# Sliding-window attention and a squared-ReLU MLP on one core: a sixth up-projection by Strassen's algorithm, softmax division on either of two engines, drawn offsets in the planner's priorities

## The chip, the cores and the metric

The kernel runs on one core of a Trainium2 chip. The metric is device microseconds for one execution. TensorE (PE in the profile) multiplies matrices into PSUM, VectorE (DVE) and ScalarE (ACT) do the elementwise work, GpSimd (POOL) issues the loads of inputs and SyncE (SP) issues transposing DMAs and stores.

## What is computed

For 8 batches, 8 heads, 576 positions and head size 64, causal attention with a window of 128 and a bias that falls off linearly with distance; its output, 4608 tokens of 512 numbers, goes through an MLP:

```python
scores = np.where(mask, scale * q @ k.T + bias, -1e9)
attn = np.exp(scores - scores.max(-1, keepdims=True))
x = (attn / attn.sum(-1, keepdims=True)) @ v       # heads side by side: 4608 x 512
h = x @ w_in                                       # 512 -> 2048
out = np.maximum(h, 0.0) ** 2 @ w_out              # 2048 -> 512
```

## The kernel before, in words

**Attention.** Each batch is cut into 5 blocks of queries (128, 128, 128, 128, 64), 40 blocks in all, numbered m. For a block the keys and queries are loaded and transposed (`prepare`), TensorE makes the scores against this block and the one before it (`scores`, line 529), ScalarE takes the exponential (line 566), VectorE multiplies by a table of masks and biases (lines 575 and 582), and TensorE multiplies by the values (`values`, line 609). The values carry a 65th column of ones, so the sum of each row's exponentials comes out beside the result. A "half" of a block is 4 heads: VectorE takes the reciprocals of the 4 sums (line 632), and `norm` multiplies the 4 x 64 columns by them (line 637), PSUM to the bf16 tile `x`. From block 13 on a DMA on SP's queue transposes `x` into the ring `xT` (line 651), which holds four groups of 512 tokens.

**MLP.** The tokens make 9 groups of 512, numbered g from 0. An up-projection of a group is either plain (`fc_step`, 16 steps of 4 matmuls with 512 columns each, line 710; ScalarE's ReLU, line 723; the square on either engine) or by Strassen's algorithm (`fast_unit`, 4 units of 7 products, each product 4 matmuls with 256 columns, line 784). Strassen's form needs sums of weight blocks (`weight_sums`, line 378, made once), sums of token blocks (`token_sums`, line 753, four subtractions into the one buffer `T`), and more elementwise work on the products: three copies by ScalarE to fp32 (lines 844, 854, 865), three additions by VectorE (lines 850 and 818), two ReLUs from PSUM by ScalarE (line 812) and two from SBUF on either engine (lines 823 and 825). `FAST` names the groups that use it: 4 to 8. The down-projections of groups 1 to 8 all go by Strassen's algorithm (`product`, 7 x 16 = 112 matmuls with 256 columns, line 935), on sums of blocks (`sums`, line 896). Group 0's is plain (line 1014).

**Order.** Nothing is ordered by hand. Each piece of work is a `Task` with a key, the engines that may take it with a cost for each, its dependencies, and the buffers and PSUM banks that it takes and frees. `Plan.order` simulates the engines: the next task is the one that can start first, with the lower priority number in front among those that can start at once (on VectorE and ScalarE, among those that can start within 100 ns of the first). A task that two engines may take goes to the one that reaches it first. The result fixes the order on each engine's queue in the program. The priority is the key plus an optional shift for the task's group (its function's name and its rounded key):

```python
t.prio = t.key + (shift.get(t.group, 0.0) if shift else 0.0)
```

Before the change `order` is called without shifts. One stage, in which the down-projection of group g runs beside the up-projection of group g + 1 and the attention for later groups, is 128 keys long. Loads of the first weights and blocks have keys below -100000; those of the later blocks about -500000.

Of the kernel before, what the change touches and what calls it, by code (L numbers as in the profile page):

```python
# [2 lines left out]

# [7 lines left out]
AF = mybir.ActivationFunctionType  # L11
# [189 lines left out]
def kernel(  # L201
    ctx: ExitStack, tc: tile.TileContext, q, k, v, moe_w_in, moe_w_out, out
):
    nc = tc.nc

    B, H, S, D = q.shape
# [3 lines left out]
    scale = 1.0 / (D ** 0.5)  # L210
# [6 lines left out]
    NG = NT // 512  # L217
# [7 lines left out]
    PLAIN = 1  # L225
    EARLY = 0.92
    WIDE = NKB
    FAST = range(NG - 5, NG)
    RING = 4 * 512

    const = ctx.enter_context(tc.tile_pool(name="const", bufs=1))
# [11 lines left out]
    def ring(name, n, shape):  # L243
        return [const.tile(shape, BF16, name=f"{name}_{i}") for i in range(n)]
# [8 lines left out]
    xt = ring("x", size["x"], [128, d_model])  # L253
    x_sums = ring("T", size["T"], [128, 3, d_model])

    plan = Plan({"rec": 4, "rt": 3, "g": 2, "S": 2, "osb": 4,
                 "s1": 1, "u2": 1, "x1": 1, "fs": 1, "fu": 2, "fx": 1, **size},
                {"h": 3, "o": 3, "a": 4, "f": 5, "t": 3})

    def bank_tile(sl, name, dtype=FP32):  # L260
        return psum.tile([128, 512 if dtype == FP32 else 1024], dtype, tag=f"bank{sl.idx}", bufs=1, name=name)

    def act(n):
        return n * 0.836 + 50.0

    def dve(n, rate=1):
        return n / rate / 0.96 + 68.0

    def mm(n):
        return max(n, 64) / 2.4 + 4.0  # L270
# [45 lines left out]
    def place(h):  # L316
        c, half = divmod(h, 2)
        return 4 * (c // 2) + 2 * half + c % 2
# [50 lines left out]
    def weight_sums(n, key):  # L369
        w = w_in_sb.rearrange("p (c k) (j r f) -> p c r k j f", c=2, r=2, f=128)  # L370
        a11, a12, a21, a22 = (w[:, c, r, :, 2 * n:2 * n + 2] for r in range(2) for c in range(2))
        s1, s2, s3, s4 = (w_sum[:, i, :, 2 * n:2 * n + 2] for i in range(4))
        last = None
        for o, a, b, op in ((s1, a21, a22, ALU.add), (s2, s1, a11, ALU.subtract),
                            (s3, a11, a21, ALU.subtract), (s4, a12, s2, ALU.subtract)):
            def emit(o=o, a=a, b=b, op=op):
                for k in range(2):
                    nc.vector.tensor_tensor(o[:, k], a[:, k], b[:, k], op=op)
            last = plan.add({"DVE": 2 * dve(256, 2)}, key, emit, [t_win[n], last, t_read[2][0]])
        t_wsum[n] = last  # L380
# [46 lines left out]
    def copy(task, o, i):  # L427
        if task.eng == "DVE":
            nc.vector.tensor_copy(o, i)
        else:  # L430
            nc.scalar.activation(o, i, AF.Copy)
# [68 lines left out]
    def bank_of(m, h):  # L500
        c, half = divmod(h, 2)
        return (0 if packed(m) else 2 * (c // 2)) + half
# [83 lines left out]
    def values(m):  # L586
        b, kb = divmod(m, NKB)
        sk, n, kb, due = prep_of[m]
        parts, sP, t_P = score_of[m]
        p0 = parts[0][0]  # L590
        first = b == 0
        x_by_dma = m >= X_DMA
        both = {"ACT": act(C * n), "DVE": dve(C * n, 2)}

        sx = Slot("x")
        t_norm = []
        for hf in range(2):
            slot_v = Slot("t")
            last = None

            def value_bank(slot_v=slot_v):
                slot_v.tile = bank_tile(slot_v, "pv")
            for hi in range(4):
                h = 4 * hf + hi
                for part, mk in parts:
                    def emit(h=h, hi=hi, part=part, mk=mk, slot_v=slot_v):
                        if slot_v.tile is None:
                            value_bank(slot_v)
                        nc.tensor.matmul(  # L609
                            slot_v.tile[:, hi * (D + 1):(hi + 1) * (D + 1)],  # L610
                            Pt[sP.idx][:, place(h), part, :], vt[s_in[mk, "v"].idx][:, h, :],
                            start=part == p0, stop=part == 1)
                    rel = []
                    if hf == 1 and hi == 3:
                        if part == 0 or kb == NKB - 1:
                            rel.append(s_in[mk, "v"])
                        if part == 1:
                            rel.append(sP)
                    new = hi == 0 and part == p0
                    last = plan.add({"PE": mm(D + 1)}, due - 12 + 4 * hf, emit,  # L620
                                    [last, t_P[bank_of(m, h)], t_in[mk, "v"]]
                                    + ([t_P[bank_of(m, 4 * hf + i)] for i in range(4)] + chain["pv"] if new else []),
                                    ([slot_v] + ([sx] if hf == 0 else [])) if new else [], rel)
                    if new:
                        last.pad = functools.partial(value_bank, slot_v), slot_v
            chain["pv"] = [last]
            srec = Slot("rec")

            def rec(slot_v=slot_v, srec=srec):
                srec.tile = work.tile([128, 4], FP32, tag="rec", bufs=4, name="rec")  # L630
                pv = slot_v.tile[:, 0:4 * (D + 1)].rearrange("p (h e) -> p h e", h=4)
                nc.vector.reciprocal(srec.tile[0:n, :], pv[0:n, :, D])
            t1 = plan.add({"DVE": 97.0}, due - 12 + 4 * hf, rec, [last], [srec])

            def norm(slot_v=slot_v, srec=srec, hf=hf):
                pv = slot_v.tile[:, 0:4 * (D + 1)].rearrange("p (h e) -> p h e", h=4)
                nc.vector.tensor_tensor(  # L637
                    xt[sx.idx][0:n, hf * 256:(hf + 1) * 256].rearrange("p (h e) -> p h e", h=4),
                    pv[0:n, :, 0:D],
                    srec.tile[0:n, :].unsqueeze(2).to_broadcast([n, 4, D]),  # L640
                    op=ALU.mult)
            t_norm.append(plan.add({"DVE": dve(256)}, due - 12 + 4 * hf, norm, [t1] + t_norm,
                                   [], [slot_v, srec]))
        t0 = b * S + kb * 128
        if x_by_dma:
            cut = [0, n] if t0 // RING == (t0 + n - 1) // RING else [0, RING - t0 % RING, n]

            def turn_x():
                for lo, hi in zip(cut, cut[1:]):
                    c0 = (t0 + lo) % RING  # L650
                    nc.sync.dma_start_transpose(xT[:, :, c0:c0 + hi - lo], xt[sx.idx][lo:hi, :])
            t_xT[b, kb] = plan.add({"SP": 1280.0 * (len(cut) - 1)}, due, turn_x, t_norm, [], [sx], dma=900.0)
        else:
            slot_x = Slot("t")
            last = None
            for c in range(C):
                def x_bank():
                    slot_x.tile = bank_tile(slot_x, "xp", BF16)

                def emit(c=c):  # L660
                    if slot_x.tile is None:
                        x_bank()
                    nc.tensor.transpose(slot_x.tile[:, c * 128:(c + 1) * 128],  # L663
                                        xt[sx.idx][:, c * 128:(c + 1) * 128], ident)
                last = plan.add({"PE": mm(128)}, due, emit, [last] + t_norm,
                                [slot_x] if c == 0 else [], [sx] if c == C - 1 else [])
                if c == 0:
                    last.pad = x_bank, slot_x

            def evac():  # L670
                copy(t_xT[b, kb], xT[:, :, t0 % RING:t0 % RING + n],
                     slot_x.tile[:, 0:512].rearrange("p (c t) -> p c t", c=C)[:, :, 0:n])
            t_xT[b, kb] = plan.add(both if first else {"DVE": both["DVE"]}, due, evac, [last], [], [slot_x])

    sk_of, t_kq_of, prep_of = {}, {}, {}
    m = 0
    while m < NBLK:
        ms = [m, m + 1] if m % NKB == NKB - 1 and MERGE <= m < NBLK - 1 else [m]
        for m in ms:
            prep_of[m] = prepare(m)  # L680
        scores(ms)
        for m in ms:
            values(m)
        m += 1
# [350 lines left out]
    for g in range(NG):  # L1035
        base = key
        if g == 2:
            for n in range(4):
                weight_sums(n, base + 64 * n)
        if g and g + 1 in FAST:  # L1040
            t_of = token_sums(g + 1, base - 60)
# [14 lines left out]
            if g * 512 < lo + blk[kb] and g * 512 + 512 > lo:  # L1056
                t.deps += t_read[g]

    done = plan.order()
    kernel.plan = done  # L1060
    with tc.manual_schedule():
        clear = 0.0
        for t in done:
            if t.eng == "PE":
                if t.start < plan.FILL and t.pad:
                    bank, slot = t.pad
                    n = round((t.start - clear) / 107.0) if t.start < plan.HOT else int(0.75 * (t.start - clear) / 56.0)
# [39 lines left out]
```

## Time and profile before

| | |
|---|---|
| median of 3 runs | 296.42 us (296.12 to 296.74) |
| the profiled execution's own time | 294.85 us |
| its span, from the first instruction to the last | 293.1 us |
| granted TensorE clock | 1.000 |
| PE, DVE, ACT busy, share of the span | 97%, 85%, 77% |

A row of the windows view gives a stretch of the span, its length, and then for each engine the busy time in it and the number of instructions, the granted clock, and the mean share of the DMA engines and what they moved. A row of a group of instructions gives line, engine, operation, output and inputs, shapes and count, then the busy time of the group and the mean duration of one in ns, then the engine's idle time ahead of them. A row of the chain that ended last gives start, length, and the work with its count. Matmuls overlap: the duration of one is longer than the distance from one to the next.

### The profile page before, as it was taken

To read this page: it belongs to the slowest core of one execution; us is meant where nothing else is said; L and a number is where in the kernel's file an instruction comes from. 1 tells how busy PE (TensorE), PEld (TensorE's weight loads), DVE (VectorE), ACT (ScalarE), POOL (GpSimd) and SP (SyncE) were. 2 spreads that over 40 slices of the span, in tenths; PEclk is the share of its full clock that TensorE was granted. 3 is DMA by queue.
4 is the path that set the end of the run, shared out by engine and by line. 5 is a ranking of instruction groups with operands and counts; after the bars stand their busy time and mean duration, and the time that the engine had idled before them with its cause. 6 is when DMAs were issued, how large, how long until landed. Compare 5 with 4: busy or idle time off the path is not lost.

```text
span 293.1 us, 8500 instructions
## 1 busy us (share of the span) xinstructions
PE 284.0 (97%) x3377; PEld 230.6 (79%) x3393; DVE 248.3 (85%) x663; ACT 227.0 (77%) x430; POOL 105.5 (36%) x131
## 2 busy tenths in 40 slices
PE   7899999999999999999999999999999999999995
PEld 6798977765666675667988888888888888888884
DVE  6967996895998757867999999899999999989923
ACT  6658998976789839878888988998889788589620
POOL 8947758824825635433714273422000000000000
PEclk9999999999999999999999999999999999999999
DMA  9999999999999999999999999999973040301223
GB/s 135 179 189 161 166 185 170 171 124 196 173 141 211 149 147 218 144 174 185 168 155 111 142 203 139 169 138 197 25 110 92 8 68 29 107 2 36 73 74 107
DMA packets 169944, 39.36 MB, mean 134 GB/s; under 512 B 157104, under 2 KB 169392, under 8 KB 169904
## 3 DMA queue, kind: packets, MB, share of 16 engines
q0 software_dynamic: 114656, 18.10, 96.8%
q1 hardware_dynamic: 54192, 20.46, 37.5%
q8 instruction: 26, 0.43, 0.6%
q10 hardware_dynamic: 1056, 0.26, 0.4%
q14 instruction: 14, 0.11, 0.2%
HBM read 36.70 MB, written 9.44 MB: 157 GB/s over the span
## 4 chain that ended last, share of the span: by engine, by line
PE 76%; DMA 12%; DVE 5%; ACT 3%; issue 2%; POOL 1%; SPq 0%; POOLq 0%; ACTq 0%
PE o L935 31%; PE f L784 19%; PE h L710 13%; DMA kq<-in_k_dram 6%; PE pv L609 5%; DMA w_in_sb<-in_moe_w_in_dram 4%; PE ps_s L529 4%; PE o L1014 4%; DMA raw<-in_k_dram 1%; ACT rt L812 1%; POOL vt L415 1%; ACT g L835 1%; DVE rt L818 1%; ACT P L566 1%; PE xp L663 1%
## 5 line engine op out<-in xcount | busy, mean ns | idle before, releaser
L566 ACT ACTIVATE P<-ps_s 128x512 bf16<-128x512 f32 (+1 forms) x130 | 68.8, 600 | 11.8 <-PE ps_s L529 11.8
L710 PE MATMUL h<-xT,w_in_sb 128*128 128x128 bf16 (+2 forms) x501 | 66.3, 270 | 1.3 <-issue 0.5
L415 POOL DMA_DIRECT2D vt<-in_v_dram x40 | 34.0, 853 | 76.6 <-PE pv L609 56.9
L935 PEld LDWEIGHTS <-g 128*128 128x128 bf16 x512 | 49.3, 98 | 8.8
L723 ACT ACTIVATE rt<-h 128x512 bf16<-128x512 f32 x64 | 37.7, 606 | 13.3 <-PE h L710 12.4
L710 PEld LDWEIGHTS <-w_in_sb 128*128 128x128 bf16 x512 | 38.7, 98 | 10.3 <-DMA w_in_sb<-in_moe_w_in_dram 0.6
L582 DVE TENSOR_TENSOR P<-P,masks 128x1024 bf16<-128x1024 bf16 x56 | 38.2, 684 | 4.2 <-ACT P L566 4.0
L935 PEld LDWEIGHTS <-S 128*128 128x128 bf16 x384 | 36.6, 98 | 6.3
L415 POOL DMA_DIRECT2D kq<-in_k_dram x39 | 33.7, 864 | 17.5 <-DMA kqT<-kq 12.1
L935 PE MATMUL o<-w_mix,S 128*128 128x256 bf16 x256 | 37.6, 273 | 0.2 <-issue 0.2
L935 PE MATMUL o<-w_out_sb,g 128*128 128x256 bf16 x256 | 37.1, 273 | 0.0
L935 PE MATMUL o<-w_mix,g 128*128 128x256 bf16 x256 | 36.9, 273 | 0.0
L784 PEld LDWEIGHTS <-w_sum 128*128 128x128 bf16 x320 | 30.9, 98 | 5.2 <-issue 0.9
L415 POOL DMA_DIRECT2D kq<-in_q_dram x39 | 33.7, 865 | 2.4 <-PE pv L609 1.2
L637 DVE TENSOR_TENSOR x<-pv,rec 128x256 bf16<-128x256 f32 (+1 forms) x80 | 33.0, 416 | 0.9
L812 ACT ACTIVATE rt<-f 128x512 bf16<-128x512 f32 x40 | 24.1, 602 | 8.5 <-PE f L784 7.5
L609 PE MATMUL pv<-vt,P 128*128 128x65 bf16 x576 | 29.6, 193 | 0.9 <-DVE P L575 0.7
L609 PEld LDWEIGHTS <-P 128*128 128x128 bf16 x576 | 25.2, 97 | 6.5 <-DVE P L575 1.5
L784 PE MATMUL f<-xT,w_in_sb 128*128 128x256 bf16 x160 | 26.0, 273 | 0.0
L784 PEld LDWEIGHTS <-w_in_sb 128*128 128x128 bf16 x240 | 22.7, 98 | 3.4
L784 PE MATMUL f<-xT,w_sum 128*128 128x256 bf16 x160 | 24.2, 272 | 0.5 <-ACT fu L854 0.5
L784 PE MATMUL f<-T,w_sum 128*128 128x256 bf16 x160 | 24.2, 272 | 0.0
(76 smaller groups left out, 475.0 us busy)
## 6 DMA issues: line engine op xcount, KB each, us to landing
out_dram<-osb SPq DMA_DIRECT2D x35, 256.0 KB, 3.8
vt<-in_v_dram POOLq DMA_DIRECT2D x32, 128.0 KB, 6.0
kq<-in_k_dram POOLq DMA_DIRECT2D x31, 128.0 KB, 6.3
kq<-in_q_dram POOLq DMA_DIRECT2D x31, 128.0 KB, 6.7
w_in_sb<-in_moe_w_in_dram POOLq DMA_DIRECT2D x4, 512.0 KB, 9.3
w_out_sb<-in_moe_w_out_dram POOLq DMA_DIRECT2D x4, 512.0 KB, 9.1
kq<-in_k_dram POOLq DMA_DIRECT2D x8, 64.0 KB, 8.1
kq<-in_q_dram POOLq DMA_DIRECT2D x8, 64.0 KB, 8.0
```

What stands on the lines that cost most here:

```text
L415: nc.gpsimd.dma_start(o, src[b, :, kb * 128:kb * 128 + n, :].rearrange("h s d -> s h d"))
L529: nc.tensor.matmul(slots[bank_of(m, 2 * c + half)].tile[:, 0:cpb * n * len(parts)].rearrange("p (c t q) -> p c t q", c=cpb, t=len(parts))[ ...
L566: nc.scalar.activation(view(Pt[sP.idx]), src, AF.Exp, bias=0.0, scale=scale)
L582: nc.vector.tensor_tensor(pt, pt, mk, op=ALU.mult)
L609: nc.tensor.matmul(slot_v.tile[:, hi * (D + 1):(hi + 1) * (D + 1)], Pt[sP.idx][:, place(h), part, :], vt[s_in[mk, "v"].idx][:, h, :], star ...
L637: nc.vector.tensor_tensor(xt[sx.idx][0:n, hf * 256:(hf + 1) * 256].rearrange("p (h e) -> p h e", h=4), pv[0:n, :, 0:D], srec.tile[0:n, :]. ...
L710: nc.tensor.matmul(slot.tile[:, f * w:(f + 1) * w], w_in_sb[:, cc, (fc + f) * 128:(fc + f + 1) * 128], xT[:, cc, g * 512 % RING + lo:g * 5 ...
L723: nc.scalar.activation(srt.tile, slot.tile, AF.Relu, bias=0.0, scale=1.0)
L784: nc.tensor.matmul(bank[name].tile[:, jj * 256:jj * 256 + 256], w, m, start=opens and jj == 0 and k == 0, stop=k == 1, skip_group_check=True)
L812: nc.scalar.activation(srt.tile, bank[name].tile, AF.Relu, bias=0.0, scale=1.0)
L935: nc.tensor.matmul(bank[t].tile[:, t * 256:(t + 1) * 256], left(g, what, j)[:, t * 128:(t + 1) * 128], right(by, j), start=opens and j == ...
L1014: nc.tensor.matmul(bank.tile, g_slots[g].tile[:, fc, t * 128:(t + 1) * 128], w_out_sb[:, fc], start=fc == 0, stop=fc == FCB - 1)
```

## The change

`FAST` begins at group 3 instead of group 4, so the up-projection of group 3 goes by Strassen's algorithm too. `norm` may be planned on ScalarE for blocks from m = 5 on: there it is four activations of 64 columns, each with a column of reciprocals as its scale, planned at 4 x (64 x 0.836 + 50) = 414 ns against 335 ns on VectorE. And each group of tasks whose rounded key is above -100000 gets a shift, drawn evenly between -8 and 8 keys with a fixed seed.

```diff
-    FAST = range(NG - 5, NG)
+    FAST = range(NG - 6, NG)
...
             def norm(slot_v=slot_v, srec=srec, hf=hf):
                 pv = slot_v.tile[:, 0:4 * (D + 1)].rearrange("p (h e) -> p h e", h=4)
+                if t_norm[hf].eng == "ACT":
+                    for h in range(4):
+                        nc.scalar.activation(xt[sx.idx][0:n, (4 * hf + h) * D:(4 * hf + h + 1) * D], pv[0:n, h, 0:D],
+                                             AF.Copy, scale=srec.tile[0:n, h:h + 1])
+                    return
                 nc.vector.tensor_tensor(
...
-            t_norm.append(plan.add({"DVE": dve(256)}, due - 12 + 4 * hf, norm, [t1] + t_norm,
+            t_norm.append(plan.add({"DVE": dve(256), "ACT": 4 * act(64)} if m >= WIDE else {"DVE": dve(256)}, due - 12 + 4 * hf, norm, [t1] + t_norm,
                                    [], [slot_v, srec]))
...
-    done = plan.order()
+    spread = random.Random(355)
+    done = plan.order({g: spread.uniform(-8.0, 8.0) for g in sorted({t.group for t in plan.tasks if t.group[1] > -100000})})
```

More of the change, by code (lines that the diff above doesn't have):

```diff
@@ L1 @@
 import functools
+import random
 from contextlib import ExitStack
```

## The prediction

> **What bounds the kernel now.** I read the page first: the busy times, then the chain of work that ended last.
>
> ```profile
> span 293.1 us, 8500 instructions
> PE 284.0 (97%) x3377; PEld 230.6 (79%) x3393; DVE 248.3 (85%) x663; ACT 227.0 (77%) x430; POOL 105.5 (36%) x131
> PE 76%; DMA 12%; DVE 5%; ACT 3%; issue 2%; POOL 1%; SPq 0%; POOLq 0%; ACTq 0%
> ```
>
> TensorE is busy for 284.0 of 293.1 us and makes 76% of the chain. The 12% of DMA are the wait for weights and first blocks (rows in the third part). Busy is not the same as full, because a matmul's recorded end lies after the next one's start. So I cut the trace into stages, at every 112th matmul of line 935 (a down-projection is 112 of them): stage g runs from the first product of group g to that of group g + 1. The windows view gives:
>
> ```profile
> core 0: us, PE busy (x) PEld busy (x) DVE busy (x) ACT busy (x) POOL busy (x), PEclk, DMA share, GB/s
> 74.60:106.20 31.60, 30.97 (x336) 21.55 (x341) 27.12 (x89) 25.03 (x47) 17.26 (x21) 1.00 1.81 170
> 106.20:137.90 31.70, 31.33 (x342) 21.05 (x345) 23.77 (x62) 24.25 (x47) 12.57 (x15) 1.00 1.96 173
> 137.90:167.30 29.40, 29.36 (x362) 25.16 (x360) 28.95 (x73) 25.28 (x49) 11.70 (x14) 1.00 1.77 142
> 167.30:197.40 30.10, 29.65 (x363) 25.23 (x361) 28.94 (x76) 26.84 (x53) 12.59 (x15) 1.00 1.67 161
> 197.40:226.70 29.30, 29.25 (x362) 25.06 (x361) 28.79 (x75) 25.95 (x51) 1.57 (x2) 1.00 0.85 108
> ```
>
> Stages 1 and 2 (31.6 and 31.7 us) hold plain up-projections, of groups 2 and 3; stages 3, 4 and 5 (29.4, 30.1, 29.3) hold Strassen's. The clock is 1.00 throughout. VectorE has 7.9 us to spare in stage 2 (31.70 - 23.77) and about 0.5 to 1.2 in stages 3 to 5; ScalarE has 7.4 us to spare in stage 2 and 3.3 to 4.1 in stages 3 to 5. To see how full TensorE is I need the distance between matmuls, which long unbroken pieces of the chain give, and the counts in each stage.
>
> ```profile
> 106.14 3.38 PE o L935 x31
> 112.73 2.16 PE h L710 x10
> 138.27 1.75 PE f L784 x16
> 70.87 0.59 PE pv L609 x16
> 70.32 0.55 PE ps_s L529 x16
> 109.53 0.56 PE ps_s L529 x24
> ```
>
> A matmul with 256 columns takes 0.109 us (3.38 / 31, and 1.75 / 16), one with 512 columns 0.216, one with values 0.037, and a burst of scores 0.55 whether it has 16 records or 24. The counts below are, in order, line 935 and line 710 in stage 2, line 784 in stage 3 (the number after PEld's busy time is complete where PE's lacks some records, and a product or two straddle a boundary), the values of line 609 in stages 2 to 5, and the scores of line 529 in stages 2 to 5.
>
> ```profile
> 106.20:137.90 31.70, 15.05 (x115) 10.52 (x113) 1.00 1.96 173
> 106.20:137.90 31.70, 16.33 (x59) 5.83 (x64) 1.00 1.96 173
> 137.90:167.30 29.40, 16.12 (x112) 10.71 (x112) 1.00 1.77 142
> 106.20:137.90 31.70, 3.52 (x72) 3.03 (x72) 1.00 1.96 173
> 137.90:167.30 29.40, 3.27 (x64) 2.86 (x64) 1.00 1.77 142
> 167.30:197.40 30.10, 3.21 (x64) 2.79 (x64) 1.00 1.67 161
> 197.40:226.70 29.30, 3.86 (x72) 3.16 (x72) 1.00 0.85 108
> 106.20:137.90 31.70, 3.12 (x96) 2.26 (x96) 1.00 1.96 173
> 137.90:167.30 29.40, 2.49 (x72) 1.81 (x72) 1.00 1.77 142
> 167.30:197.40 30.10, 2.49 (x72) 1.80 (x72) 1.00 1.67 161
> 197.40:226.70 29.30, 2.27 (x64) 1.64 (x64) 1.00 0.85 108
> ```
>
> The 96 scores are 3 bursts of 16 and 2 of 24, the 72 are 3 and 1, the 64 are 4 and none. Stage 2 then needs 112 x 0.109 + 64 x 0.216 + 72 x 0.037 + 5 x 0.55 = 12.2 + 13.8 + 2.7 + 2.75 = 31.45 us of its 31.7. Stage 3 needs 12.2 + 12.2 + 2.4 + 2.2 = 29.0 of 29.4, stage 4 the same of 30.1, stage 5 12.2 + 12.2 + 2.7 + 2.2 = 29.3 of 29.3. So TensorE's own work is the bound; unfilled are 0.25, 0.4, 1.1 and 0 us, 1.75 us in these four stages.
>
> **The change, first part: group 3 by Strassen.** Stage 2 loses 64 matmuls of 0.216 (13.8 us) and gets 112 of 0.109 (12.2): -1.6 us of TensorE, needing 29.85. This lies on the path that sets the end. What could take it back is the elementwise work, for VectorE and ScalarE then carry what they carry in stages 3 to 5, where VectorE is all but full. Those stages leave 0.4, 1.1 and 0 us unfilled, 0.5 on average, so I take 30.35 for stage 2, which is **-1.35 us**; with 0 unfilled it is -1.85, with 1.1 -0.75.
>
> Two steps are moved with it. The weight sums are now needed at about 106 us rather than 138. The token sums of group 3 are four more subtractions, which stand between the landing of its last tokens and its first product; those of group 4 can no longer run ahead, because `T` is then held by group 3.
>
> ```profile
> L378 DVE TENSOR_TENSOR w_sum<-w_in_sb,w_sum x8: 276/285/285, 79.8 to 89.5; 128x256 bf16<-128x256 bf16 x8
> L753 DVE TENSOR_TENSOR T<-xT,T x10: 413/417/423, 133.4 to 253.2; 128x512 bf16<-128x512 bf16 x10
> 105.60 3.93 PE o L935 x36
> POOL vt L415 <- PE pv L609: 56.9, 14, 8.4
> ```
>
> The weight sums are done by 90 us: 16 us of cover, no cost. The token sums are not so well covered: from 105.60 on TensorE runs 36 down-projection products in a row, with no up-projection between them, so group 3's tokens come just in time, and 4 x 0.417 = 1.7 us are added behind them. The cover is the 112 products of group 2, of which 76 would still be left; I cost it at nothing, and at +1.7 us if the cover runs out (first part then +0.3). That the loads could not follow speaks little: GpSimd waited 56.9 us for value buffers that TensorE had yet to free, so input waits for TensorE and not the other way.
>
> **Second part: the division on ScalarE.** No row of before shows an activation of 64 columns or one with a column as its scale. Nearest are exponentials from PSUM, in the timeline and in the groups by shape, and VectorE's form of the step:
>
> ```profile
> 6.85 1.21 ACT L566 ACTIVATE P<-ps_s 128x256 bf16<-128x256 f32 x4
> 10.19 2.06 ACT L566 ACTIVATE P<-ps_s 128x512 bf16<-128x512 f32 x4 [1.64 <-PE ps_s L529]
> L566 ACT ACTIVATE P<-ps_s 128x512 bf16<-128x512 f32 x126 | 67.6, 606 | 11.8 <-PE ps_s L529 11.8
> L566 ACT ACTIVATE P<-ps_s 128x256 bf16<-128x256 f32 x4 | 1.2, 398 | 0.0
> L637 DVE TENSOR_TENSOR x<-pv,rec 128x256 bf16<-128x256 f32 x64 | 26.7, 419 | 0.8
> 167.30:197.40 30.10, 4.15 (x10) 1.00 1.67 161
> ```
>
> From one start to the next: (1.21 - 0.398) / 3 = 0.27 us at 256 columns, (2.06 - 0.606) / 3 = 0.485 at 512. The line through them gives 0.11 at 64; the durations give 0.242 (398 - 192 x 208 / 256). So a division on ScalarE costs between 4 x 0.11 = 0.44 us, near its planned price, and 4 x 0.242 = 0.97 us, if nothing overlaps. I take 0.44, since the rows of one line do overlap, and keep 0.97. The last row above is line 637 in stage 4: 10 divisions. If half move, VectorE gains 5 x 0.42 = 2.1 us and ScalarE gets 2.2 more, inside its 3.3 us. On the path this can return at most the 1.75 us unfilled; VectorE's 28.94 of 30.1 in stage 4 says that it is part of the reason there, and I take **-0.3**. A new wait comes with it: ScalarE's activation waits for VectorE's reciprocal, and behind it in ScalarE's queue stand exponentials, for which VectorE's masks and then the values wait, and ReLUs and copies, for whose banks TensorE waits. The price of a bad wait is in the third part.
>
> The Trainium skill speaks against this step ("ScalarE: Activation LUTs", section "What ACT_TABLE_LOAD costs"): each operand that is a column costs about 93 ns more per activation. By that, as an estimate, four cost 4 x (0.11 + 0.093) = 0.81 us; five take 4.05 us, 0.75 over in stage 4 and 0.7 in stage 5, and the sum would come to +0.1, 296.5 us. No row of before shows it, and the sum does without it; as a mechanism it is rival (a) below.
>
> **Third part: the drawn shifts.** A stage of 31.7 us is 128 keys, so 8 keys are 2.0 us. Nothing is added or removed; what moves is the order of ready work on all engines, with SP's transposes and stores. The loads on GpSimd's queue, with keys below -100000, keep their numbers. The first 47 us are paced by such loads:
>
> ```profile
> 12.38 12.83 DMA w_in_sb<-in_moe_w_in_dram
> 36.60 9.83 DMA kq<-in_k_dram
> 275.01 14.64 PE o L935 x134
> ```
>
> The end is a plain row of 134 products, which no order shortens. Between them a better order can win back the 1.75 us unfilled in stages 2 to 5 and little elsewhere, and a worse one can bring each block's values or transposed tokens up to 2 us late. I take **0**, with -1.5 and +3.
>
> **The sum**: -1.35 - 0.3 + 0 = -1.65, rounded to -1.7 us: the span goes from 293.1 to 291.4, the profiled execution from 294.85 to 293.15. That execution lies 1.57 us below the median of 296.42, and the same difference on the median gives **294.7 us**.
>
> **Rivals.** (a) ScalarE becomes the bound: at 0.97 us each, five divisions take 4.85 us. ScalarE has 4.1, 3.3 and 3.35 us spare in stages 3 to 5, and about 4.3 in stage 2 once it carries Strassen's work (30.35 less the mean of the other three, 26.0). With five in each it is over by 0.75, 1.55, 1.5 and 0.55, 4.35 us, all handed to TensorE by exponentials and copies that come late: -1.35 + 4.35 = +3.0, **299.4 us**, slower. It decides from 0.66 us per division on (3.3 / 5). For it: the planner's price has no room for a column operand. Against: ScalarE's other flexible work can go to VectorE in return. (b) The gain doesn't arrive: group 3's tokens come late and the four subtractions behind them stay uncovered, +1.7 against -1.35 - 0.3, **296.4 us**. For it: the 36 products in a row at 105.60. Against: 76 products are left, and stages 3 to 5 begin with token sums too. (c) The order falls well, -1.5 more: **293.2 us**. (d) It falls badly, +3: **297.7 us**; for it, VectorE's spare half microsecond in stages 3 and 5; against, the planner still lets no ready engine idle by its own account.
>
> **How the numbers follow.** Forecast 0.43, (a) 0.17, (b) 0.14, (c) 0.18, (d) 0.08. The range is 292.9 to 298.0: it takes in the forecast, (b), (c), (d) and the half of (a) where the price lies nearer its lower end, and leaves out about 0.15. About 0.2%, 0.6 us, is what a measurement of this kernel can tell from no change. Faster by more than that: forecast and (c), 0.61; within: (b), 0.14; slower: (a) and (d), 0.25. The forecast's own range is 294.0 to 295.6.
>
> **What would show it.** Stage 2, cut as above, at 30.35 us with 112 matmuls on line 784 and none on line 710; stages 3 to 5 as long as before or 0.3 us shorter in sum. Divisions on ScalarE: four starts within about 0.44 us; at over 0.66 (a) is alive, and then ScalarE's busy time fills stages 4 and 5. For (b) a longer unbroken row of line 935 at 105 us and a gap on TensorE after it. For (c) and (d) a difference in stages that the first two parts don't touch: before 74.6 us and after 226.7. The prediction is wrong if stage 2 stays above 31.2 us or the first 74.6 us change by more than 1.

## The result and the profile after

The changed kernel takes 303.69 us (median of 4 runs, 303.11 to 305.11) beside 296.27: 1.0266 of the time before by the means of the runs, with a 95% interval of 1.0215 to 1.0316. The prediction was 294.7 us, faster. The profiled execution took 303.89 us. From its page, the busy times and the chain that ended last:

```profile
span 302.0 us, 8751 instructions
PE 288.6 (96%) x3429; PEld 235.3 (78%) x3441; DVE 252.7 (84%) x657; ACT 250.5 (83%) x572; POOL 105.8 (35%) x131
PE 35%; ACT 35%; DMA 14%; DVE 8%; issue 4%; POOL 3%; ACTq 0%; POOLq 0%
```

TensorE's share of the chain fell from 76% to 35%, ScalarE's rose from 3% to 35%. Cut into stages as before (stages 1 to 5; the columns are those of the windows shown there):

```profile
76.10:108.20 32.10, 31.57 (x335) 21.45 (x340) 27.22 (x87) 26.58 (x63) 17.25 (x21) 1.00 1.95 169
108.20:139.20 31.00, 30.23 (x378) 25.35 (x377) 28.39 (x70) 27.81 (x65) 11.70 (x14) 1.00 1.70 158
139.20:171.10 31.90, 30.84 (x370) 25.36 (x368) 29.03 (x75) 31.58 (x81) 12.67 (x15) 1.00 1.55 150
171.10:203.40 32.30, 31.04 (x371) 25.74 (x370) 28.61 (x70) 30.89 (x79) 12.60 (x15) 1.00 1.55 149
203.40:234.60 31.20, 30.33 (x362) 25.18 (x361) 29.15 (x74) 29.61 (x77) 1.57 (x2) 1.00 0.54 94
```

Stage 2 did get shorter, 31.7 to 31.0 us. But stages 3, 4 and 5, which hold Strassen's up-projections in both kernels, went from 29.4, 30.1 and 29.3 us to 31.9, 32.3 and 31.2, 6.6 us in sum. (Of the 8.9 us between the two profiled spans, the stretch ahead of stage 1 has +1.5, stage 1 +0.5, stage 2 -0.7, stages 3 to 5 +6.6 and stage 6 +1.0.) In stage 3 ScalarE is busy for 31.58 of 31.9 us. The shares by line of the chain through these three stages, and then the group of the new instructions from the page, name the work:

```profile
by line: ACT x L640 17.3%; ACT P L567 12.4%; ACT rt L818 10.2%; ACT g L841 8.1%; issue 6.9%; PE f L790 6.5%; ACT rt L831 5.9%; PE o L941 5.5%; DMA kqT<-kq 5.2%; ACT fs L850 3.4%; ACT fx L871 3.4%; ACT fu L860 3.3%; DVE P L583 1.9%; DVE rt L
```

```profile
L640 ACT ACTIVATE x<-pv,rec 128x64 bf16<-128x64 f32 (+1 forms) x144 | 33.9, 353 | 3.4 <-DVE rec L633 3.2
```

144 activations are 36 divisions on ScalarE. They fill 33.9 us, 0.94 us for each division by busy time. Stages 3, 4 and 5 have 28 activations each, that is seven divisions:

```profile
139.20:171.10 31.90, 6.68 (x28) 1.00 1.55 150
171.10:203.40 32.30, 6.64 (x28) 1.00 1.55 149
203.40:234.60 31.20, 6.81 (x28) 1.00 0.54 94
```

In the timeline a division and what follows it:

```profile
146.31 0.97 ACT L640 ACTIVATE x<-pv,rec 64x64 bf16<-64x64 f32 x4
147.09 0.67 ACT L871 ACTIVATE fx<-f 128x512 f32<-128x512 f32 x1
```

The copy behind it starts 147.09 - 146.31 = 0.78 us after the division's start: that is what a division costs the queue, 0.195 us for each activation (the median distance between neighbouring starts over the trace is 197 ns). The plan has 0.41 us for it.

### The profile page after: what moved, and what is told of

Read it like the earlier page. It is cut to its first block, busy times and chain, and to the rows that moved or that the text cites. A ratio compares the mean times of both kernels' runs of the same rounds, so it can differ in the third digit from the quotient of the medians.

```text
span 302.0 us, 8751 instructions
## 1 busy us (share of the span) xinstructions
PE 288.6 (96%) x3429; PEld 235.3 (78%) x3441; DVE 252.7 (84%) x657; ACT 250.5 (83%) x572; POOL 105.8 (35%) x131
## 4 chain that ended last, share of the span: by engine, by line
PE 35%; ACT 35%; DMA 14%; DVE 8%; issue 4%; POOL 3%; ACTq 0%; POOLq 0%
PE o L941 14%; PE f L790 9%; DMA kq<-in_k_dram 8%; ACT x L640 8%; ACT P L567 7%; ACT rt L818 5%; PE h L716 5%; PE o L1020 4%; DMA w_in_sb<-in_moe_w_in_dram 4%; ACT g L841 4%; ACT rt L831 3%; DVE P L583 2%; ACT fx L871 2%; ACT fu L860 2%; PE pv L610 2%
## 5 line engine op out<-in xcount | busy, mean ns | idle before, releaser
L567 ACT ACTIVATE P<-ps_s 128x512 bf16<-128x512 f32 (+1 forms) x130 | 71.8, 631 | 5.9 <-PE ps_s L530 5.7
L716 PE MATMUL h<-xT,w_in_sb 128*128 128x128 bf16 (+2 forms) x442 | 50.8, 256 | 1.6 <-DMA w_in_sb<-in_moe_w_in_dram 1.0
L790 PEld LDWEIGHTS <-w_sum 128*128 128x128 bf16 x384 | 36.9, 97 | 7.5 <-issue 2.1
L716 PEld LDWEIGHTS <-w_in_sb 128*128 128x128 bf16 x448 | 32.9, 98 | 7.2 <-DMA w_in_sb<-in_moe_w_in_dram 1.4
L729 ACT ACTIVATE rt<-h 128x512 bf16<-128x512 f32 x48 | 27.9, 606 | 12.0 <-PE h L716 9.2
L640 ACT ACTIVATE x<-pv,rec 128x64 bf16<-128x64 f32 (+1 forms) x144 | 33.9, 353 | 3.4 <-DVE rec L633 3.2
L818 ACT ACTIVATE rt<-f 128x512 bf16<-128x512 f32 x48 | 30.2, 633 | 4.3 <-PE f L790 4.1
L790 PEld LDWEIGHTS <-w_in_sb 128*128 128x128 bf16 x288 | 27.4, 97 | 6.3 <-issue 2.1
L790 PE MATMUL f<-xT,w_in_sb 128*128 128x256 bf16 x192 | 29.9, 272 | 0.3 <-ACT fs L850 0.3
L790 PE MATMUL f<-T,w_sum 128*128 128x256 bf16 x192 | 29.2, 272 | 0.6 <-ACT osb L432 0.3
L790 PE MATMUL f<-xT,w_sum 128*128 128x256 bf16 x192 | 28.7, 272 | 0.1
```

The lines of the kernel that those rows point to most:

```text
L567: nc.scalar.activation(view(Pt[sP.idx]), src, AF.Exp, bias=0.0, scale=scale)
L640: nc.scalar.activation(xt[sx.idx][0:n, (4 * hf + h) * D:(4 * hf + h + 1) * D], pv[0:n, h, 0:D], AF.Copy, scale=srec.tile[0:n, h:h + 1])
L716: nc.tensor.matmul(slot.tile[:, f * w:(f + 1) * w], w_in_sb[:, cc, (fc + f) * 128:(fc + f + 1) * 128], xT[:, cc, g * 512 % RING + lo:g * 5 ...
L729: nc.scalar.activation(srt.tile, slot.tile, AF.Relu, bias=0.0, scale=1.0)
L790: nc.tensor.matmul(bank[name].tile[:, jj * 256:jj * 256 + 256], w, m, start=opens and jj == 0 and k == 0, stop=k == 1, skip_group_check=True)
L818: nc.scalar.activation(srt.tile, bank[name].tile, AF.Relu, bias=0.0, scale=1.0)
```

## The experiments

"Plan" below is the end of TensorE's last task by the kernel's own planner, against 289.8 us for the kernel before; "chip" is the ratio of times, formed from means, so it can differ a little from that of the medians. Each kernel ran beside the kernel before on the same chip.

| | Strassen groups | division | shifts | plan | chip, 95% interval | median, us |
|---|---|---|---|---|---|---|
| changed kernel | six | either, at 0.41 | seed 355 | -1.9 | 1.0266 (1.0215-1.0316) | 303.69 |
| e1 | six | VectorE | seed 355 | +2.2 | 1.0110 (1.0088-1.0133) | 299.30 |
| e2 | six | either, at 0.41 | none | +0.9 | 1.0282 (1.0243-1.0321) | 304.12 |
| e3 | six | VectorE | none | +2.8 | 1.0116 (1.0084-1.0148) | 299.55 |
| e4 | six | either, constant scale | seed 355 | -1.9 | 0.9969 (0.9947-0.9992) | 295.50 |
| e5 | five | either, at 0.41 | none | -0.7 | 1.0114 (1.0080-1.0148) | 299.69 |
| e6 | five | VectorE | seed 355 | +1.9 | 1.0055 (1.0029-1.0081) | 298.48 |
| e7 | six | either, at 0.79 | seed 355 | +1.7 | 1.0086 (1.0046-1.0126) | 298.62 |
| e8 | six, early tokens | VectorE | none | +1.0 | 1.0030 (1.0001-1.0060) | 297.18 |
| e9 | five | either, constant scale | none | -0.7 | 0.9969 (0.9943-0.9996) | 294.99 |
| e10 | five | VectorE | small, drawn anew | -0.9 | 0.9965 (0.9937-0.9992) | 295.24 |
| e11 | five | either, at 0.79 | small, drawn anew | -0.8 | 0.9969 (0.9943-0.9996) | 295.05 |

**e1, e2, e3: parts taken out.**

```diff
-            t_norm.append(plan.add({"DVE": dve(256), "ACT": 4 * act(64)} if m >= WIDE else {"DVE": dve(256)}, due ...
+            t_norm.append(plan.add({"DVE": dve(256)}, due ...        # e1, e3
-    done = plan.order({g: ...})
+    done = plan.order()                                          # e2, e3
```

> The changed kernel with the division planned on VectorE alone; six Strassen up-projections and the drawn shifts stay. Theory P (price: an activation of 64 columns with a column as its scale takes 197 ns from start to start in the changed kernel's trace, so a division takes 0.79 us on ScalarE where the plan has 0.41, and ScalarE falls behind its plan): the loss is gone, 294 to 296 us. Theory S (the shifts spoil the order): still slow, 300 us or more. Theory W (the sixth Strassen up-projection itself fills VectorE and ScalarE): 298 us or more.

> The changed kernel without the shifts; six Strassen up-projections and the division on either engine stay. Theory P: as slow as the changed kernel, 301 to 305 us, with about as many divisions on ScalarE (36) at 0.79 us each. Theory S: the loss is gone, 294 to 296. Theory W: 298 us or more.

> Six Strassen up-projections alone: no shifts, and the division on VectorE alone. Theories P and S: the first part's own worth, 1.35 us below the kernel before, 294.9 us (294.4 to 295.7). Theory W: slower than before, 298 us or more.

e2 fits theory P: without the shifts the loss is all there, though with 29 divisions on ScalarE and not the 36 that were expected. But e1 and e3 go against theory P: with the division back on VectorE 3.3 and 3.4 us remain, so the sixth Strassen up-projection costs by itself, as theory W has it. The planner's own account has most of that: +2.8 us for e3. e3's stages 2 and 3, and a stretch inside stage 2:

```profile
106.70:140.90 34.20, 32.68 (x386) 26.47 (x385) 29.98 (x76) 26.27 (x52) 11.70 (x14) 0.95 1.76 156
140.90:172.20 31.30, 30.32 (x375) 25.36 (x372) 30.65 (x79) 26.40 (x51) 12.58 (x15) 1.00 1.52 147
...
106.70:114.00 7.30, 7.26 (x99) 6.00 (x98) 5.63 (x14) 3.70 (x8) 0.23 (x1) 1.00 1.70 147
114.00:118.00 4.00, 4.00 (x44) 3.56 (x40) 2.70 (x10) 2.46 (x5) 3.71 (x5) 1.00 1.58 238
118.00:122.00 4.00, 4.00 (x48) 3.29 (x46) 3.96 (x11) 3.73 (x8) 2.87 (x4) 1.00 1.87 145
122.00:126.00 4.00, 2.85 (x28) 1.87 (x25) 3.96 (x11) 4.00 (x9) 0.00 (x0) 1.00 2.43 165
126.00:130.00 4.00, 3.67 (x35) 2.62 (x36) 4.00 (x13) 3.88 (x9) 1.12 (x2) 0.64 1.42 137
```

Until 118 us VectorE and ScalarE have time to spare (busy for 8.3 and 6.2 of 11.3 us); from 118 to 130 both are all but full, and from 122 to 126 TensorE waits (2.85 of 4). The chain from 116.5 to 127.7 us runs on ScalarE for nine tenths:

```profile
by line: ACT rt L818 24.7%; ACT P L567 15.9%; ACT g L841 14.7%; ACT fu L860 9.8%; ACT rt L831 8.9%; ACT fs L850 8.8%; DVE f L856 6.3%; ACT fx L871 4.4%; issue 4.2%; ACT x L432 2.5%; ACTq L850 0.2%
```

Two rows say when group 3's token sums and first products came; the first of the two start times in each row is group 3's:

```profile
L759 DVE TENSOR_TENSOR T<-xT x6: 416/418/419, 109.2 to 255.9; 128x512 bf16<-128x512 bf16 x6
L790 PE MATMUL f<-T,w_sum x192: 269/272/282, 114.6 to 275.0; 128*128 128x256 bf16 x192
```

The four subtractions begin at 109.2, and the first product that needs them runs at 114.6, 8 us into the stage. In the kernel before, the chain has matmuls of group 3's plain up-projection from 4.6 us into the stage on:

```profile
110.79 1.46 PE h L710 x6
```

Not all of the 34.2 us is waiting: the granted clock in this execution's stage 2 was 0.95, which is worth up to 34.2 x 0.05 = 1.7 us. The loss of e3 as a whole doesn't hang on it: the three of its four runs with a clock of 0.998 or more took 298.51 to 300.42 us.

**e8: the tokens early.** Group 3's up-projection reads group 2's tokens (`gg`), and `b12` of that copy goes to a tile of its own.

```diff
+        gg = 2 if g == 3 else g
-        x = xT[:, :, g * 512 % RING:g * 512 % RING + 512]...
+        x = xT[:, :, gg * 512 % RING:gg * 512 % RING + 512]...
```

> Six Strassen up-projections alone, as in the third experiment, but the up-projection of group 3 reads the tokens of group 2, which are there some 30 us earlier; so the output for group 3's tokens is computed from group 2's, the work is the same in amount. Theory T (group 3's tokens and their four subtractions come 7 us into stage 2, and the elementwise work of Strassen's form is crammed into what is left): most of the 3.4 us come back, 296 to 297.5 us, and stage 2 falls from 34.2 us below 32.5. Theory W (VectorE and ScalarE can't carry it wherever it starts): 299 us or more, stage 2 at 34 us.

```profile
106.70:138.60 31.90, 30.68 (x387) 25.65 (x385) 27.97 (x69) 27.50 (x53) 11.80 (x14) 1.00 1.91 162
138.60:169.50 30.90, 30.12 (x371) 25.54 (x368) 29.94 (x79) 27.12 (x53) 12.63 (x15) 1.00 1.80 152
```

Stage 2 falls from 34.2 to 31.9 us; how much of that is the clock, which is 1.00 here, can't be told from these rows. The times can be compared: all ten runs of e8 have a clock of 0.998 or more and took 296.29 to 298.38 us, and of the 3.4 us some 2.5 come back (1.0116 to 1.0030, each known to about 0.9 us), where the plan has 1.8. Theory T holds for most of the loss; the planner orders everything anew around the early tokens, so this is the worth of their being early with that order. The rest stays with stages 2 and 3 although the tokens are there: stage 2 takes 31.9 us where TensorE needs 29.85, and stage 3 takes 30.9 where the kernel before took 29.4. Why is not shown.

**e4 and e9: the same order, the column operand gone.**

```diff
-                                             AF.Copy, scale=srec.tile[0:n, h:h + 1])
+                                             AF.Copy)
```

> The changed kernel with every instruction in the same order, but the activations that divide on ScalarE have the constant scale 1 instead of the column of reciprocals; so the division by the sums is left out where it is planned on ScalarE (36 halves of blocks), and the rest is computed. Theory P in its narrow form (the column operand is what the plan had no price for): starts about 103 ns apart instead of 197, a division 0.41 us as planned, and the time falls to 294 to 297 us. If a small activation costs about 190 ns whatever its scale: no change, 302 to 305 us. Theory S: 300 us or more, with starts 103 ns apart.

> The second part alone, as in the fifth experiment and with every instruction in the same order, but the activations that divide on ScalarE have the constant scale 1; so the division by the sums is left out in those 25 halves of blocks. Theory P: starts 103 ns apart instead of 197, and the 3.3 us that the part costs by itself are gone, 295 to 296.5 us. If the part costs by its waits between engines: 298.5 us or more.

> The kernel before with the second part alone: the division on either engine, planned at 0.41 us on ScalarE; five Strassen up-projections, no shifts. Theory P (the column operand makes each division 0.79 us): about 25 divisions on ScalarE hold it 25 x 0.37 = 9 us longer than planned, most of it after 137 us where ScalarE has 3 to 4 us a stage to spare; slower, 298.5 to 301 us. Theory X (the price hurts only together with the sixth Strassen up-projection): 295.5 to 297 us.

e5 is the second part alone on the kernel before: at 299.69 us it comes out as theory P has it, and theory X, by which the price hurts only together with the first part, is out. e9 is to e5 what e4 is to the changed kernel. In each pair the order on every engine is the same, and ScalarE still waits for the reciprocals (3.2 us ahead of the divisions in the changed kernel, 3.0 in e4). In e4's timeline the division that was shown above, and then its stages 2 to 4:

```profile
145.60 0.53 ACT L640 ACTIVATE x<-pv 64x64 bf16<-64x64 f32 x4
146.08 0.60 ACT L871 ACTIVATE fx<-f 128x512 f32<-128x512 f32 x1
```

```profile
109.50:139.50 30.00, 29.74 (x378) 25.42 (x377) 28.24 (x70) 26.91 (x66) 11.72 (x14) 1.00 1.69 161
139.50:169.40 29.90, 29.86 (x371) 25.44 (x369) 29.02 (x75) 29.28 (x80) 12.58 (x15) 1.00 1.63 158
169.40:199.30 29.90, 29.90 (x370) 25.46 (x368) 28.20 (x69) 28.64 (x79) 12.57 (x15) 1.00 1.68 161
```

0.48 us instead of 0.78 to the next start here (median 103 ns from start to start), and the time goes from 303.7 to 295.5 us; between e5 and e9 from 299.7 to 295.0. TensorE is again busy all through stages 3 and 4. So it is the column operand, 94 ns per activation, and nothing else about the division on ScalarE, that took 8.2 us from the changed kernel and 4.7 from e5. The groups of e5 and e9 (mean duration behind the comma, in ns) show the same operand:

```profile
L640 ACT ACTIVATE x<-pv,rec 128x64 bf16<-128x64 f32 x92 | 21.5, 336 | 1.0 <-DVE rec L633 0.8
```

```profile
L640 ACT ACTIVATE x<-pv 128x64 bf16<-128x64 f32 x92 | 13.3, 242 | 1.1 <-DVE rec L633 0.7
```

336 - 242 = 94 ns.

**e6: the shifts alone; e7: the right price.**

```diff
-    done = plan.order()
+    done = plan.order({g: spread.uniform(-8.0, 8.0) ...})        # e6, on the kernel before
-"ACT": 4 * act(64)}
+"ACT": 4 * 197.0}                                                # e7, on the changed kernel
```

> The kernel before with the third part alone: the drawn shifts; five Strassen up-projections, the division on VectorE alone. Theory N (a draw that suits one set of costs is just a random disturbance for another): slower by some 2 us, 297 to 299 us, spread over stages 2 to 5. Theory O (the order hardly matters where TensorE is full): 295.6 to 297 us.

> The changed kernel with one number altered: the planner is told 4 x 197 = 788 ns for a division on ScalarE instead of 414. All three parts stay. Theory P: ScalarE keeps to its plan, and most of the 7.4 us come back; the sixth Strassen up-projection without cheap divisions still costs, so 297 to 299 us. If the divisions hurt for another reason than their price in the plan (a wait between engines, a bank held longer): 301 us or more, as long as some 30 divisions are still on ScalarE.

The shifts alone cost 0.55%, 1.6 us, near the 2 us of theory N but not spread over stages 2 to 5. The plan has 1.5 us of it in stage 4, and there the profiled execution has 31.5 us instead of 30.1:

```profile
169.90:201.40 31.50, 30.19 (x377) 25.92 (x377) 30.35 (x78) 28.47 (x56) 12.57 (x15) 1.00 1.79 154
```

e7 has 31 divisions on ScalarE, nearly as many as the changed kernel, and is 5 us faster: planned at its price, the division does little harm. What remains, 2.5 us, is within 0.9 of the plan's own +1.7.

**e10 and e11: small shifts drawn under right prices.** Each takes the one of 300 seeds whose plan ends earliest.

```diff
-    done = plan.order()
+    spread = random.Random(191)                                  # e11: 231, and 4 * 197.0 for ScalarE
+    done = plan.order({g: spread.uniform(-1.5, 1.5) ...})
```

> Five Strassen up-projections and the division on VectorE alone, as before, with shifts between -1.5 and 1.5 keys drawn with another seed, the one of 300 that ends earliest by the planner's own account (0.85 us ahead of the kernel before). If the account holds where all its prices are right: faster by 0.5 to 1.0 us, 295.3 to 295.9 beside 296.4. If it doesn't resolve such differences: within 0.5 us of the kernel before, on either side.

> Five Strassen up-projections, the division on either engine with the price of 788 ns on ScalarE (32 of 80 there by the plan), and shifts between -1.5 and 1.5 keys drawn with the seed of 300 that ends earliest by the planner's own account (0.8 us ahead of the kernel before). If the price was all that was wrong with the division on ScalarE: faster by 0.3 to 1.0 us. If divisions on ScalarE cost beyond their price (waits between engines, banks held longer): slower than the kernel before by 1 us or more.

Both come out ahead of the kernel before, by 0.35% and 0.31%, with intervals that end just below 1. e10's stages 3 to 5, in a profiled execution that was the fastest of its twelve (293.30 us beside a median of 295.24):

```profile
137.40:166.70 29.30, 29.30 (x362) 25.13 (x361) 28.74 (x73) 25.19 (x49) 11.69 (x14) 1.00 1.59 144
166.70:196.00 29.30, 29.30 (x363) 25.16 (x361) 28.68 (x76) 27.12 (x54) 12.57 (x15) 1.00 1.61 163
196.00:225.20 29.20, 29.20 (x361) 25.06 (x360) 28.16 (x74) 26.23 (x52) 1.56 (x2) 1.00 0.76 108
```

Stage 4 gives up 0.8 of the 1.1 us that it had unfilled before. e11 has 32 divisions on ScalarE: with the price right, they cost nothing that these intervals, about 0.8 us either way, can show.

## Why the prediction was wrong

The sign was wrong. By the steps:

- **Second part, the step "I take 0.44, since the rows of one line do overlap".** The activations do overlap, but each column operand adds 94 ns, and a division costs 0.79 us. Rival (a) was right, with its point of decision at 0.66 us: 36 divisions hold ScalarE 36 x 0.38 = 14 us longer than planned, and without the operand the kernel is 8.2 us shorter (e4). The rows that were extrapolated have constants as their scale, so they could not show the operand's price. The Trainium skill ("ScalarE: Activation LUTs", section "What ACT_TABLE_LOAD costs") gives about 93 ns for it; by that the prediction's estimate was 0.81 us for a division, and the trace agrees at 0.79. "If half move", five divisions in a stage, was too few as well: the planner moved seven in each of stages 3 to 5. By the prediction's own figures, 7 x 0.79 = 5.5 us against 4.1, 3.3 and 3.35 us to spare on ScalarE leave 1.4, 2.2 and 2.2 over, 5.8 us in sum; the three stages grew by 6.6. The predicted +0.1 us behind it missed, because it had five divisions in a stage, handed ScalarE's excess to TensorE in two stages only and kept -1.35 for the first part.
- **First part, the step "The cover is the 112 products of group 2, of which 76 would still be left; I cost it at nothing".** The cover lasted for TensorE's time but not for VectorE's and ScalarE's: they had 3.0 and 5.1 of 11.3 us to spare until 118 us and were then full with Strassen's elementwise work. -1.35 was measured at +3.4 (e3). Late tokens are some 2.5 us of it (e8), so rival (b) had the cause, if not the path, for it looked for a gap on TensorE right behind the down-projection; the analogy with stages 3 to 5 ("0.5 on average" unfilled) fails for the rest, about 0.9 over the kernel before and 2.3 over the forecast, which was not taken apart further. The planner, which could have been asked before any run, has +2.8 us for this part alone. That the part does pay once VectorE is relieved at the planned price, e4 shows: stage 2 at 30.0 us, where 30.35 was forecast.
- **Third part, taken at 0 with -1.5 and +3.** Measured +1.6 (e6), inside its bounds. The prediction didn't ask under which prices the draw is good: the plan has the changed kernel 1.9 us ahead at 0.41 us for a division, and 1.7 us behind with the same seed when the division is at its price (e7); on the kernel before, with the division on VectorE, the seed puts it 1.9 us behind (e6).
- Right were the account of TensorE (1.6 us fewer, stage 2 at 30.0 when nothing else binds), rival (a)'s mechanism and sign of it ("ScalarE's busy time fills stages 4 and 5", 30.89 of 32.3 and 29.61 of 31.2, and stage 3 above all).
- One of the prediction's own signs of being wrong came true: the stretch ahead of stage 1 changed by more than 1 us, from 74.6 to 76.1. Its cause stays open (last section).
- The sum of the parts alone, 3.4 + 3.4 + 1.6 = 8.4 us, is near the whole, 7.4 by medians.

## What to carry to other kernels

Where a planner orders the work and the bounding engine is full, an alternative on a second engine is worth what its price in the plan is worth: measure the very form of the instruction, operands and all, before it is offered. A drawn order fits the prices that the plan was made with, and can turn against the kernel when one is wrong (e6 and e7 by the plan, with e6 measured alone at +1.6 us); e10 and e11 show what a choice among 300 draws gives when the prices are right, a third of a per cent. And before work is moved to a faster algorithm in an earlier stage, look at when its inputs land: time in which the helper engines idle at the start is taken from the time that they need at the end.

## What the runs showed of the hardware

A column as the scale of an activation costs ScalarE 94 ns more each time (197 instead of 103 ns from start to start at 64 columns). With a constant in its place the order on every engine is the same and ScalarE's wait for the reciprocals stays, so the difference is the operand's.

In e3's profile the granted TensorE clock fell to 0.64 from 126 to 130 us, right after 4 us in which TensorE was busy for 2.85, with no single wait longer than 1.0 us (the row has the total, the number of waits and the longest):

```profile
PE pv L610 <- DVE P L583: 1.2, 2, 1.0
```

The profiled executions of e1 and e2 have the same at the same place: busy for 3.37 and 3.01 of the 4 us from 122 on, then a clock of 0.68 and 0.76. In e3, 3.24 of 4 us (158 to 162) were not followed by a lower clock. What decides is not shown. The clock of e3's execution was 0.994 on the whole, and another run of e3 had 1.000 and 300.42 us, so it isn't what makes e3 slow.

The stretch ahead of stage 1 took between 74.2 us (e10) and 77.9 (e4) in the profiled executions, one of each kernel; e4 has the same order as the changed kernel, which took 76.1, so the parts alone don't set it. What does stays open, and no conclusion above rests on it.
